# Attention and FFN in one kernel: FFN units as 64-row halves beside the 64-row score matmuls, one run per slot

## Chip, cores and metric

One core of one Trainium2 chip. The metric is the device time of one execution in microseconds (us), median of several runs.

## The reference

```python
scores = q @ k.T / 8 + bias[bucket(|i-j|)]      # B=8, H=8, S=576, D=64
attn   = softmax(scores)
x      = (attn @ v) as [4608, 512]
out    = ((x @ w_a) * (x @ w_b)) @ w_out        # 512 -> 1536 -> 512
```

Scores have a contraction of only 64 (the head size). 576 rows are 4 x 128 and a tail of 64.

## The kernel before

Two heads are one *pair*; the 32 pairs are processed in 32 *slots*. Into each slot are woven *units* of the FFN, each of four full matmuls of 128 rows and 512 columns: unit a (`pa`), unit b (`pb`), and a third of an output tile (`po`).

```python
def qk1(p, t):                      # two heads side by side: rows 0-63 and rows 64-127
    ps = ps_sc.tile([128, 2, 512], FP32, tag="sc")          # 2 buffers, 2 banks each
    for hh in range(2):
        r = slice(64 * hh, 64 * hh + 64)
        nc.tensor.matmul(out=ps[:, hh, :], lhsT=kT_(p, t)[r, :], rhs=qT[r, :, :], start=True, stop=True)

def qk_tail(p):                     # scores of the tails: full 128 rows, the other head padded with zeros
    for t in range(4):
        nc.tensor.matmul(out=ps[:, 0, :]..., lhsT=kT_(p, t), rhs=qTt_(p))            # 128 columns
    nc.tensor.matmul(out=ps[:, 1, :], lhsT=kTt_(p), rhs=qT_(p))                      # 512 columns
    pt = bank(TR if p < R3 else AV)                                                  # small tail scores, 64 columns

# a slot from 12 on ("unit" stands for a share of the slot's nine):
steps = [qk1(s,0)+qk1(s,1), ex(s,0), unit, ex(s,1), av 0-2 of s-1, norm, unit, mul(s,0), unit, mul(s,1),
         av 3-4 of s-1, norm, ..., qk1(s,2)+qk1(s,3), ex(s,2), unit, ex(s,3), unit, mul(s,2), unit, mul(s,3),
         qk_tail(s), ex_tail(s), unit, unit, mul_tail(s), unit]
```

`ex` is the exponential on ScalarE, `mul` the multiplication by the exponentiated bias on VectorE, `av` attention times v, `norm` the reciprocal and the division (`rc`, `XG`) on VectorE. From slot 12 on both av groups and the small tail scores share one bank ("av", one buffer). FFN results take two banks "ffn" and one "tr".

The softmax here doesn't subtract the row's maximum and nothing guards it: scores larger than these inputs give would overflow.

## Time and profile before

| | before |
|---|---|
| median time | 418.04 us (417.79 to 418.82, 4 runs) |
| slot length, slots 12 to 31 | 11.06 us each |
| TensorE busy / ScalarE / VectorE | 98% / 59% / 47% |
| visits to the 64-row form per slot | 2 |

The lines themselves are in the prediction. The view that carries most is the chain of waits: the work that ended last, followed back through what released each piece.

### The profile page before, as it was taken

To read this page: it belongs to the slowest core of one execution; us is meant where nothing else is said; L and a number is where in the kernel's file an instruction comes from. 1 tells how busy PE (TensorE), PEld (TensorE's weight loads), DVE (VectorE), ACT (ScalarE), POOL (GpSimd) and SP (SyncE) were. 2 spreads that over 40 slices of the span, in tenths; PEclk is the share of its full clock that TensorE was granted. 3 is DMA by queue.
4 is the path that set the end of the run, shared out by engine and by line. 5 is a ranking of instruction groups with operands and counts; after the bars stand their busy time and mean duration, and the time that the engine had idled before them with its cause. 6 is when DMAs were issued, how large, how long until landed. Compare 5 with 4: busy or idle time off the path is not lost.

```text
span 415.9 us, 8484 instructions
## 1 busy us (share of the span) xinstructions
PE 406.9 (98%) x3407; PEld 208.1 (50%) x3407; DVE 197.0 (47%) x484; ACT 246.1 (59%) x347; POOL 119.4 (29%) x161
## 2 busy tenths in 40 slices
PE   8799999999999999999999999999999999999996
PEld 3563555555454555554554455555545554444443
DVE  3684666556542555355525563455425540430430
ACT  4887476756656766577666665676567642322321
POOL 9898739903538000920073003000000000000000
PEclk9999999999999999999999999999999999999999
DMA  9999999999939950999099908921120002002004
GB/s 160 190 155 179 159 171 145 183 165 87 140 51 168 176 44 22 155 188 103 16 115 199 124 16 74 177 48 39 41 90 7 11 17 101 2 0 102 2 0 101
DMA packets 164935, 40.75 MB, mean 98 GB/s; under 512 B 155320, under 2 KB 160224, under 8 KB 164896
## 3 DMA queue, kind: packets, MB, share of 16 engines
q0 software_dynamic: 110448, 18.75, 61.9%
q1 hardware_dynamic: 53168, 21.03, 26.8%
q10 hardware_dynamic: 1280, 0.43, 0.5%
q8 instruction: 26, 0.43, 0.4%
q14 instruction: 13, 0.11, 0.1%
HBM read 38.77 MB, written 9.45 MB: 116 GB/s over the span
## 4 chain that ended last, share of the span: by engine, by line
PE 92%; DVE 2%; POOL 2%; DMA 1%; ACT 1%; issue 1%; DVEq 0%; POOLq 0%; ACTq 0%
PE pa L511 23%; PE pb L511 23%; PE po L542 22%; PE av L412 9%; PE qk L342 7%; PE av L403 2%; PE qkt L367 2%; PE qkt L370 2%; DMA W<-bias_tab 1%; DVE XG L449 1%; DVE at L361 1%; PE po L530 1%; PE trx L475 1%; PE qktt L373 0%; PE trq L291 0%
## 5 line engine op out<-in xcount | busy, mean ns | idle before, releaser
L353 ACT ACTIVATE at<-qk 128x1024 bf16<-128x1024 f32 x128 | 125.9, 1023 | 24.4 <-PE qk L342 23.4
L523 DVE TENSOR_TENSOR g<-pb,ha 128x512 bf16<-128x512 f32 x108 | 74.7, 692 | 117.0 <-PE pb L511 102.9
L511 PE MATMUL pa<-xn,wa 128*128 128x512 bf16 x432 | 111.3, 380 | 0.2 <-DVE xn L257 0.2
L511 PE MATMUL pb<-xn,wb 128*128 128x512 bf16 x432 | 111.2, 379 | 0.0
L518 ACT ACTIVATE ha<-pa 128x512 f32<-128x512 f32 x108 | 64.6, 598 | 65.4 <-PE pa L511 64.9
L542 PE MATMUL po<-wo,g 128*128 128x512 bf16 x420 | 98.6, 379 | 0.0
L511 PEld LDWEIGHTS <-wa 128*128 128x128 bf16 x432 | 39.1, 98 | 49.6 <-issue 9.3
L511 PEld LDWEIGHTS <-wb 128*128 128x128 bf16 x432 | 39.2, 98 | 48.1 <-issue 7.6
L361 DVE TENSOR_TENSOR at<-at,W 128x512 bf16<-128x512 bf16 (+1 forms) x128 | 59.1, 484 | 7.7 <-ACT at L353 5.5
L542 PEld LDWEIGHTS <-g 128*128 128x128 bf16 x420 | 37.9, 98 | 46.4 <-issue 7.4
L546 ACT ACTIVATE ob<-po 128x512 f32<-128x512 f32 x35 | 20.9, 597 | 60.7 <-PE po L542 60.7
L123 POOL DMA_DIRECT2D vm<-in_v_dram x32 | 28.2, 924 | 99.4 <-PE av L412 61.2
L412 PE MATMUL av<-vm,at 128*128 128x65 bf16 x992 | 43.5, 193 | 0.0
L412 PEld LDWEIGHTS <-at 128*128 128x128 bf16 x992 | 39.5, 97 | 6.3
L448 DVE RECIPROCAL rc<-av 128x6 f32<-128x6 f32 x64 | 12.0, 188 | 54.9 <-PE av L412 53.1
L403 PE MATMUL av<-vt,att 128*128 128x130 bf16 x156 | 34.7, 222 | 0.0
L381 ACT ACTIVATE att<-qkt 128x1024 bf16<-128x1024 f32 x32 | 32.6, 1020 | 0.0
L449 DVE TENSOR_TENSOR XG<-av,rc 128x384 bf16<-128x384 f32 x64 | 31.4, 491 | 2.4 <-DVE rc L448 0.2
L123 POOL DMA_DIRECT2D qn<-in_q_dram x28 | 24.4, 921 | 24.6 <-PE trq L291 24.6
L123 POOL DMA_DIRECT2D kn<-in_k_dram x28 | 24.5, 913 | 4.9 <-DMA vt<-in_v_dram 2.0
L342 PE MATMUL qk<-QTb,KTb 64*128 64x512 bf16 x160 | 24.2, 381 | 0.0
L403 PEld LDWEIGHTS <-att 128*128 128x128 bf16 x156 | 15.3, 98 | 7.4 <-issue 0.7
(122 smaller groups left out, 243.6 us busy)
## 6 DMA issues: line engine op xcount, KB each, us to landing
out_dram<-ob SPq DMA_DIRECT2D x32, 256.0 KB, 4.1
vm<-in_v_dram POOLq DMA_DIRECT2D x28, 128.0 KB, 5.5
qn<-in_q_dram POOLq DMA_DIRECT2D x24, 128.0 KB, 8.5
kn<-in_k_dram POOLq DMA_DIRECT2D x24, 128.0 KB, 9.3
wa<-in_moe_w_a_dram POOLq DMA_DIRECT2D x3, 512.0 KB, 6.8
wb<-in_moe_w_b_dram POOLq DMA_DIRECT2D x3, 512.0 KB, 9.5
wo<-in_moe_w_out_dram POOLq DMA_DIRECT2D x1, 1536.0 KB, 13.2
W<-bias_tab POOLq DMA_DIRECT2D x4, 192.0 KB, 5.8
```

The lines of the kernel that those rows point to most:

```text
L123: nc.gpsimd.dma_start(out=(vm[b % 2][:, h0:h1, t, 0:Dh] if dst is None else dst[b % 2][:, :].rearrange("p (t h d) -> p t h d", h=H, t=NM)[ ...
L342: nc.tensor.matmul(out=ps[:, hh, :], lhsT=kT_(p, t)[r, :], rhs=qT[r, :, :], start=True, stop=True)
L353: nc.scalar.activation(out=at[:, :, :], in_=ps[:, :, :], func=ACTF.Exp, scale=scale)
L361: nc.vector.tensor_tensor(out=at[:, :, lo:hi], in0=at[:, :, lo:hi], in1=w[:, :, y:(None if z < 0 else z):-1], op=MULT)
L381: nc.scalar.activation(out=at[:, 0:1024].rearrange("p (a x) -> p a x", a=2), in_=ps[:, :, :], func=ACTF.Exp, scale=scale)
L403: nc.tensor.matmul(out=pav[:, slot, :, :], lhsT=x, rhs=vt[b // 2 % 2][:, 4 * i + hp, :, 0:Dh + 1], start=fresh, stop=True, skip_group_chec ...
L412: nc.tensor.matmul(out=pav[:, slot, hh, :], lhsT=x, rhs=vm[i][:, 2 * hp + hh, t, 0:Dh + 1], start=False, stop=True, skip_group_check=True)
L449: nc.vector.tensor_tensor(out=xg[:, j0:j0 + n, :, :], in0=pav[:, 0:n, :, 0:Dh], in1=rc.unsqueeze(3).to_broadcast([128, n, 2, Dh]), op=MULT)
L511: nc.tensor.matmul(out=ff[key][:, :], lhsT=w[df // FW][:, mc, 128 * (df % FW):128 * (df % FW) + 128], rhs=xn_sb[mc][:, xin(c)], start=(i = ...
L518: nc.scalar.activation(out=ha[:, :], in_=ff["pa"][:, :], func=ACTF.Copy)
L523: nc.vector.tensor_tensor(out=g_sb[df][:, :], in0=ff["pb"][:, :], in1=ff["ha"][:, :], op=MULT)
L542: nc.tensor.matmul(out=po[:, :], lhsT=g_sb[df][:, 128 * tt:128 * tt + 128], rhs=wo_sb[:, df, :], start=(df == 0), stop=(df == NDF - 1))
```

## The change

The intent: each change between the full form and the 64-row form of TensorE costs time. If FFN matmuls are themselves cut into 64-row halves, and halves of two different units run side by side, they can stand among the qk pairs without a change of form.

```diff
+    R4 = 14
-    g_sb = [wpool.tile(...) for df in range(NDF)]
+    g_sb = [[wpool.tile(...) for df in range(NDF)] for i in range(2)]     # two sets of activations
     def qk_tail(p):
+        if p >= R4:                        # tails in row halves, no zero half streamed
+            for t in range(NM):
+                for hh in range(2):
+                    nc.tensor.matmul(out=ps[:, hh, 64*t:64*t+64], lhsT=kT_(p, t)[r, :], rhs=qTt_(p)[r, ...])
+            for x in range(2):
+                nc.tensor.matmul(out=ps[:, x, 256:512], lhsT=kTt_(p), rhs=qT_(p)[:, 2*x:2*x+2, :])
...
+    def begin(x, y):                       # unit x rows 0-63 beside unit y rows 64-127
+        for p, q_ in zip(*got):
+            mm(p, lo); mm(q_, hi)
+        nc.vector.tensor_copy(out=hop, in_=got[1][0][0][0:1, 0:1])        # orders the two halves
+    def end(x, y, got):                    # then the other halves
+        for p, q_ in zip(*got):
+            mm(q_, lo, False, True, True); mm(p, hi, False, True, True)
+        u_end(y[0]); u_end(x[0])
+    def run(s, a, b):
+        u, v_ = ((b[0], FF), (a[0], AV)), ((b[1], FF), (a[1], TR))
+        qk1(s, 0); ex(s, 0); got0 = begin(*u)
+        qk1(s, 1); ex(s, 1); got1 = begin(*v_)
+        qk1(s, 2); ex(s, 2); end(*u, got0)
+        qk1(s, 3); ex(s, 3); end(*v_, got1)
...
-    quotas = {4: 12, 5: 7, 6: 6, 7: 4, 8: 4}
+    quotas = {4: 12, 5: 7, 6: 6, 7: 4, 8: 4, 12: 3, 13: 3}               # units of a slot; otherwise 9
+        elif new and s >= R4:
+            c, i = (s - 6) // 4, 3 * ((s - R4) % 4)
+            a, b = [[(kind, c, i + j, 0) for j in range(3)] for kind in "ab"]
+            mine = [u for u in outs if u[1] < c][0:3]                     # empty in slots 16 and 17
+            steps += [run, qk_tail, mine[0:1], ex_tail, mul 0, mine[1:2], mul 1, av 0-2, norm,
+                      a[2:], mul 2, mine[2:], av 3-4, norm, t_x, turns, b[2:], mul 3, mul_tail]
```

(Cuts marked with dots, the last list in short form; there is also one output buffer fewer, three instead of four. `hop` is a copy of one element between the first and the second halves of an accumulation, so that the second come after the first.)

More of the change, by code (lines that the diff above doesn't have):

```diff
@@ L48 @@
     wrk = ctx.enter_context(tc.tile_pool(name="wrk", bufs=2))
-    obp = ctx.enter_context(tc.tile_pool(name="obp", bufs=4))
+    obp = ctx.enter_context(tc.tile_pool(name="obp", bufs=3))
     atp = ctx.enter_context(tc.tile_pool(name="atp", bufs=8))
@@ L115 @@
     xn_sb = [wpool.tile([128, 3 * SM + ST * B], BF16, name=f"xn{mc}") for mc in range(NMC)]
-    g_sb = [wpool.tile([128, DM], BF16, name=f"g{df}") for df in range(NDF)]
+    g_sb = [[wpool.tile([128, DM], BF16, name=f"g{i}_{df}") for df in range(NDF)] for i in range(2)]
     def early(b):
@@ L365, in qk_tail @@
         ps = ps_sc.tile([128, 2, 512], FP32, tag="sc", name=f"qkt{p}")
-        for t in range(NM):
+        if p >= R4:
+            for t in range(NM):
+                for hh in range(2):
+                    r = slice(64 * hh, 64 * hh + 64)
+                    nc.tensor.matmul(out=ps[:, hh, ST * t:ST * t + ST], lhsT=kT_(p, t)[r, :],
+                                     rhs=qTt_(p)[r, ST * hh:ST * hh + ST], start=True, stop=True)
+            for x in range(2):
+                nc.tensor.matmul(out=ps[:, x, 256:512], lhsT=kTt_(p), rhs=qT_(p)[:, 2 * x:2 * x + 2, :],
+                                 start=True, stop=True)
+        for t in range(NM if p < R4 else 0):
             nc.tensor.matmul(
@@ L369, in qk_tail @@
                 lhsT=kT_(p, t), rhs=qTt_(p), start=True, stop=True)
-        nc.tensor.matmul(out=ps[:, 1, :], lhsT=kTt_(p), rhs=qT_(p), start=True, stop=True)
+        if p < R4:
+            nc.tensor.matmul(out=ps[:, 1, :], lhsT=kTt_(p), rhs=qT_(p), start=True, stop=True)
         pt = bank(TR if p < R3 else AV, FP32, f"qktt{p}")
@@ L380, in ex_tail @@
         nc.scalar.activation(out=at[:, 1024:1024 + ST], in_=pt[:, 0:ST], func=ACTF.Exp, scale=scale)
-        nc.scalar.activation(out=at[:, 0:1024].rearrange("p (a x) -> p a x", a=2),
-                             in_=ps[:, :, :], func=ACTF.Exp, scale=scale)
+        if p < R4:
+            nc.scalar.activation(out=at[:, 0:1024].rearrange("p (a x) -> p a x", a=2),
+                                 in_=ps[:, :, :], func=ACTF.Exp, scale=scale)
+        else:
+            nc.scalar.activation(out=at[:, 0:1024].rearrange("p (y a x) -> p a y x", y=2, a=2),
+                                 in_=ps[:, :, :].rearrange("p a (y x) -> p a y x", y=2),
+                                 func=ACTF.Exp, scale=scale)
     def mul_tail(p):
@@ L494 @@
     turn3 = 0
+    here = None
+    hop = const.tile([1, 1], FP32, name="hop")
     def ff_bank(name):
         nonlocal turn3
-        where = FF
-        if ring3:
+        where = here or FF
+        if ring3 and here is None:
             turn3 += 1
@@ L504, with ff_in, mm, a_end @@
     MC = (0, 1, 2, 3)
-    def ff_mm(c, df, w, key, m0, m1):
-        if m0 == 0:
-            ff[key] = ff_bank(f"{key}{c}_{df}")
-        for i in range(m0, m1):
-            mc = MC[i]
-            nc.tensor.matmul(out=ff[key][:, :], lhsT=w[df // FW][:, mc, 128 * (df % FW):128 * (df % FW) + 128],
-                             rhs=xn_sb[mc][:, xin(c)],
-                             start=(i == 0), stop=(i == NMC - 1))
-    def ff_a(c, df, m0=0):
-        ff_mm(c, df, wa_sb, "pa", m0, NMC)
-        ha = wrk.tile([128, 512], FP32, tag="ha", name=f"ha{c}_{df}")
-        nc.scalar.activation(out=ha[:, :], in_=ff["pa"][:, :], func=ACTF.Copy)
-        ff["ha"] = ha
-    def ff_b(c, df, m0=0):
-        ff_mm(c, df, wb_sb, "pb", m0, NMC)
-        nc.vector.tensor_tensor(out=g_sb[df][:, :], in0=ff["pb"][:, :], in1=ff["ha"][:, :], op=MULT)
+    def ff_in(c, df, w, key):
+        if (key, df) not in ff:
+            ff[key, df] = ff_bank(f"{key}{c}_{df}")
+        return [(ff[key, df], w[df // FW][:, mc, 128 * (df % FW):128 * (df % FW) + 128],
+                 xn_sb[mc][:, xin(c)], i == 0, i == NMC - 1) for i, mc in enumerate(MC)]
+    lo, hi = slice(0, 64), slice(64, 128)
+    def mm(x, r=slice(0, 128), start=None, stop=None, go_on=False):
+        o, w, m, first, final = x
+        return nc.tensor.matmul(out=o[:, :], lhsT=w[r, :], rhs=m[r, :],
+                         start=first if start is None else start,
+                                stop=final if stop is None else stop, skip_group_check=go_on)
+    def a_end(c, df):
+        ha = wrk.tile([128, 512], FP32, tag="ha", name=f"ha{c}_{df}")
+        nc.scalar.activation(out=ha[:, :], in_=ff.pop(("pa", df))[:, :], func=ACTF.Copy)
+        ff["ha", df] = ha
+    def b_end(c, df):
+        nc.vector.tensor_tensor(out=g_sb[c % 2][df][:, :], in0=ff.pop(("pb", df))[:, :], in1=ff.pop(("ha", df))[:, :], op=MULT)
     def ff_last(c, tt):
@@ L529, in ff_last @@
             for df in range(NDF):
-                nc.tensor.matmul(out=po[:, cols], lhsT=g_sb[df][:, 128 * tt:128 * tt + 128],
+                nc.tensor.matmul(out=po[:, cols], lhsT=g_sb[c % 2][df][:, 128 * tt:128 * tt + 128],
                                  rhs=wo_sb[:, df, cols], start=(df == 0), stop=(df == NDF - 1))
@@ L535, in ff_last, with ff_out @@
                 eng.dma_start(out=out[r0:r0 + ST, cols], in_=ob[64 * hh:64 * hh + 64, cols])
-    def ff_o(c, tt, part):
+    def ff_out(c, tt, part):
         if part == 0:
-            ff["po"] = ff_bank(f"po{c}_{tt}")
-        po = ff["po"]
-        for df in range(4 * part, 4 * part + 4):
-            nc.tensor.matmul(out=po[:, :], lhsT=g_sb[df][:, 128 * tt:128 * tt + 128],
-                             rhs=wo_sb[:, df, :], start=(df == 0), stop=(df == NDF - 1))
-        if part == 2:
-            ob = obp.tile([128, DM], FP32, tag="ob", name=f"ob{c}_{tt}")
-            nc.scalar.activation(out=ob[:, :], in_=po[:, :], func=ACTF.Copy)
-            if c < B:
-                r0 = S * c + 128 * tt
-                nc.sync.dma_start(out=out[r0:r0 + 128, :], in_=ob[:, :])
-            else:
-                for hh in range(2):
-                    r0 = S * (2 * tt + hh) + SM
-                    nc.sync.dma_start(out=out[r0:r0 + ST, :], in_=ob[64 * hh:64 * hh + 64, :])
+            ff["po", tt] = ff_bank(f"po{c}_{tt}")
+        return [(ff["po", tt], g_sb[c % 2][df][:, 128 * tt:128 * tt + 128], wo_sb[:, df, :], df == 0, df == NDF - 1)
+                for df in range(4 * part, 4 * part + 4)]
@@ new lines, in o_end @@
+    def o_end(c, tt, part):
+        if part < 2:
+            return
+        po = ff.pop(("po", tt))
+        ob = obp.tile([128, DM], FP32, tag="ob", name=f"ob{c}_{tt}")
+        nc.scalar.activation(out=ob[:, :], in_=po[:, :], func=ACTF.Copy)
+        if c < B:
+            r0 = S * c + 128 * tt
+            nc.sync.dma_start(out=out[r0:r0 + 128, :], in_=ob[:, :])
+        else:
+            for hh in range(2):
+                r0 = S * (2 * tt + hh) + SM
+                nc.sync.dma_start(out=out[r0:r0 + ST, :], in_=ob[64 * hh:64 * hh + 64, :])
@@ L555 @@
     units = []
-    def last(part):
-        if part == 0:
-            ff_last(NCH - 1, 3)
     for c in range(NCH):
         for df in range(NDF):
-            m0 = 3 if c == 0 and df == 0 else 0
-            units.append(lambda c=c, df=df, m0=m0: ff_a(c, df, m0))
-            units.append(lambda c=c, df=df, m0=m0: ff_b(c, df, m0))
+            units.append(("a", c, df, 0))
+            units.append(("b", c, df, 0))
         for tt in range(4):
             for part in range(3):
-                if c == NCH - 1 and tt == 3:
-                    units.append(lambda part=part: last(part))
-                else:
-                    units.append(lambda c=c, tt=tt, part=part: ff_o(c, tt, part))
+                units.append(("o", c, tt, part))
@@ L571, with u_mms, u_end @@
     nxt = 0
+    def u_mms(u):
+        kind, c, i, part = u
+        if kind == "o":
+            return ff_out(c, i, part)
+        mms = ff_in(c, i, wa_sb if kind == "a" else wb_sb, "pa" if kind == "a" else "pb")
+        return mms[3:] if c == 0 and i == 0 else mms
+    def u_end(u):
+        kind, c, i, part = u
+        if kind == "a":
+            a_end(c, i)
+        elif kind == "b":
+            b_end(c, i)
+        else:
+            o_end(c, i, part)
     def put_units(n):
@@ L575, in put_units, with put_in @@
         for _ in range(n):
-            units[nxt]()
+            u = units[nxt]
             nxt += 1
+            if u[0] == "o" and u[1] == NCH - 1 and u[2] == 3:
+                if u[3] == 0:
+                    ff_last(NCH - 1, 3)
+                continue
+            for x in u_mms(u):
+                mm(x)
+            u_end(u)
+    def put_in(us, where):
+        nonlocal here
+        for u in us:
+            here = where
+            for x in u_mms(u):
+                mm(x)
+            here = None
+            u_end(u)
+    def begin(x, y):
+        nonlocal here
+        got = []
+        for u, where in (x, y):
+            here = where
+            got.append(u_mms(u))
+        here = None
+        for p, q_ in zip(*got):
+            mm(p, lo)
+            mm(q_, hi)
+        nc.vector.tensor_copy(out=hop[:, :], in_=got[1][0][0][0:1, 0:1])
+        return got
+    def end(x, y, got):
+        for p, q_ in zip(*got):
+            mm(q_, lo, False, True, True)
+            mm(p, hi, False, True, True)
+        u_end(y[0])
+        u_end(x[0])
+    def run(s, a, b):
+        u, v_ = ((b[0], FF), (a[0], AV)), ((b[1], FF), (a[1], TR))
+        qk1(s, 0)
+        ex(s, 0)
+        got0 = begin(*u)
+        qk1(s, 1)
+        ex(s, 1)
+        got1 = begin(*v_)
+        qk1(s, 2)
+        ex(s, 2)
+        end(*u, got0)
+        qk1(s, 3)
+        ex(s, 3)
+        end(*v_, got1)
     ACT = nc.scalar
@@ L714 @@
     norm(3, 3)
-    ff_mm(0, 0, wa_sb, "pa", 0, 3)
+    for x in ff_in(0, 0, wa_sb, "pa")[0:3]:
+        mm(x)
     t_x(3, AV, range(3))
     t_x(3, AV, range(3, 5))
-    ff_mm(0, 0, wb_sb, "pb", 0, 3)
+    for x in ff_in(0, 0, wb_sb, "pb")[0:3]:
+        mm(x)
     copy(ACT, xn_sb[3][:, 0:384], st[3]["x"][:, 0:384])
@@ L737, in turns @@
             turn(b, "qkt"[s % 4])
-    quotas = {4: 12, 5: 7, 6: 6, 7: 4, 8: 4}
+    quotas = {4: 12, 5: 7, 6: 6, 7: 4, 8: 4, 12: 3, 13: 3}
+    outs = None
+    every = list(units)
     for s in range(4, NP + 1):
@@ L745 @@
         steps = []
+        if s == R4:
+            outs = [("o", c, tt, part) for c in range(1, NCH) for tt in range(4) for part in range(3)]
+            outs = outs[3 * (R4 - R3):]
         if s == R3:
@@ L754 @@
                       lambda: t_k(5, AV), lambda: c_k(5), U, U]
+        elif new and s >= R4:
+            c, i = (s - 6) // 4, 3 * ((s - R4) % 4)
+            a, b = [[(kind, c, i + j, 0) for j in range(3)] for kind in "ab"]
+            mine = [u for u in outs if u[1] < c][0:3]
+            outs = outs[len(mine):]
+            steps += [lambda: run(s, a, b), lambda: qk_tail(s), lambda: put_in(mine[0:1], FF), lambda: ex_tail(s),
+                      lambda: mul(s, 0), lambda: put_in(mine[1:2], FF), lambda: mul(s, 1), A(0, 1, 2), N(0),
+                      lambda: put_in(a[2:], TR), lambda: mul(s, 2), lambda: put_in(mine[2:], FF), A(3, 4), N(3),
+                      lambda: t_x(s - 1), lambda: turns(s), lambda: put_in(b[2:], FF),
+                      lambda: mul(s, 3), lambda: mul_tail(s)]
         elif new:
@@ L780 @@
         quota = quotas.get(s, 9)
+        if s == NP:
+            c, i = (s - 6) // 4, 3 * ((s - R4) % 4)
+            units = [u for u in outs if u[1] < c] + [u for u in units if u[1] == c and u[0] < "o" and u[2] >= i]
+            units += [u for u in outs if u[1] == c]
+            for d in range(c + 1, NCH):
+                units += [u for u in every if u[1] == d]
+            nxt = 0
         seen, put = 0, 0
```

## The prediction

> **What bounds the kernel now.** I read the page first (busy shares, slices, chain), then the chain of waits between two head-pair slots, then the timelines of the four engines there.
>
> ```profile
> PE 406.9 (98%) x3407; PEld 208.1 (50%) x3407; DVE 197.0 (47%) x484; ACT 246.1 (59%) x347; POOL 119.4 (29%) x161
> ...
> PE   8799999999999999999999999999999999999996
> ...
> PE 92%; DVE 2%; POOL 2%; DMA 1%; ACT 1%; issue 1%; DVEq 0%; POOLq 0%; ACTq 0%
> ```
>
> TensorE is busy 98% of the span, from the third slice to the last but one, and 92% of the chain that ended last is TensorE. The busy share alone proves little, because the recorded matmuls overlap (a 512-column matmul is recorded as 379 ns, but the next starts 216 ns later). So I turn to the chain, whose pieces are start-to-start times. This is one slot (one pair of heads plus nine FFN units), slot 14:
>
> ```profile
> 138.47 0.54 PE qk L342 x4
> 139.01 0.97 PE pa L511 x4
> ...
> 140.03 0.24 PE av L412 x8
> ...
> 143.20 0.54 PE qk L342 x4
> 143.74 0.97 PE pb L511 x4
> 144.71 0.86 PE pa L511 x4
> ...
> 146.44 0.22 PE qkt L367 x4
> 146.66 0.22 PE qkt L370
> 146.88 0.06 PE qktt L373 x2
> ...
> 149.53 0.54 PE qk L342 x4
> ```
>
> Columns: start, length, what. Every piece is PE, with nothing of another engine between: in this stretch TensorE waits for nobody. A slot lasts 149.53 - 138.47 = 11.06 us, and the other slots up to 31 begin at the same 11.06 us step. A unit of four full matmuls costs 0.86 (4 x 0.216), but 0.97 when it follows qk: 0.11 is lost. The four qk matmuls run as two concurrent 64-row pairs, which should cost 2 x 0.216 = 0.43, and cost 0.54: again 0.11. So each visit to the 64-row form costs 0.21-0.22 us, and a slot has two of them.
>
> The other engines in the same slot (timelines: start, length, engine, line, what; in brackets the idle time before):
>
> ```profile
> 142.64 0.60 ACT L518 ACTIVATE ha<-pa 128x512 f32<-128x512 f32 x1 [1.12 <-PE pa L511]
> 143.57 1.94 ACT L353 ACTIVATE at<-qk 128x1024 bf16<-128x1024 f32 x2 [0.33 <-PE qk L342]
> ...
> 146.97 0.22 ACT L380 ACTIVATE att<-qktt 128x64 bf16<-128x64 f32 x1 [0.76 <-PE qktt L373]
> 147.09 1.02 ACT L381 ACTIVATE att<-qkt 128x1024 bf16<-128x1024 f32 x1
> ```
> ```profile
> 140.91 0.20 DVE L448 RECIPROCAL rc<-av 128x6 f32<-128x6 f32 x1 [1.64 <-PE av L412]
> 141.14 0.56 DVE L449 TENSOR_TENSOR XG<-av,rc 128x384 bf16<-128x384 f32 x1
> 141.85 0.69 DVE L523 TENSOR_TENSOR g<-pb,ha 128x512 bf16<-128x512 f32 x1
> 142.46 0.88 DVE L361 TENSOR_TENSOR at<-at,W 128x512 bf16<-128x512 bf16 x2
> ```
>
> Both have gaps, so neither bounds. What I take from them: exps of 1.02 us follow each other at 0.92 (1.94 for two), so an instruction overlaps the next by about 0.1; the av bank is free about 1.1 us after the last av matmul (av 0-2 streams until 140.87 on the chain's clock, the last matmul starting near 140.68; reciprocal at 140.91, XG to 141.70); an exp starts 0.43 us after its qk pair (records: qk at 143.14, exp at 143.57).
>
> **What the Trainium skill says.** "TensorEngine Tiling (Array Packing)", Key Properties: changing the tiling mode, not just the tile, drains the engine. The trace agrees: 0.11 us on each side. "TensorE: Matmul & The Clock Gate", Part 3: matmuls in different row groups run concurrently, their starts some 4 ns apart. The trace agrees: qk x4 of 512 columns takes 0.54, not 0.86. "Perfetto Trace Analysis", Identifying the Most-Contended Engine, says that matmul busy time is a poor measure because matmuls are pipelined; this trace shows it (379 ns recorded, 216 from start to start). "TensorEngine Tiling (Array Packing)", Gotcha 1, says that different row tiles cannot access the same PSUM bank at once; the change gives each half of a pair its own bank, as qk already does, and no run here shows the other case.
>
> **The change, part by part** (18 slots, 14 to 31).
>
> 1. One visit to the 64-row form per slot instead of two. The run is qk, four unit pairs, qk, four, qk, four, qk, four, and the tail's 64-row part follows directly; then comes full form until the next run. Units in halves: 16 full matmuls become 32 halves = 16 concurrent pairs at 0.216, the same array time (that a pair keeps 0.216 in a run of 20 is taken from runs of two; nothing in this trace is longer). Saved: 18 x 0.21 = 3.8 us.
>
> 2. Tail scores: four full matmuls with zero-padded heads (0.22) become four concurrent pairs of 64 columns. Matmuls of 64-65 columns start 0.03 apart (av x8 in 0.24, qktt x2 in 0.06), so four pairs take 0.13 if pairs overlap, 0.24 if the weight loads do not. The 512-column one becomes two of 256: the same. Saved: up to 18 x 0.09 = 1.7 us; I take 1.6.
>
> So TensorE's own work would give 418.2 - 5.4 = 412.8, with steady slots of 11.06 - 0.30 = 10.76.
>
> 3. What comes back as waits. The units are redistributed: slots 12 and 13 get three instead of nine, slots 16 and 17 have six (no output unit is allowed while the previous chunk is used up), the rest go to the end, which is TensorE alone at the same 0.86 a unit. Moving work costs nothing, but the thin slots lose their filler.
>
> Slots 12 and 13, from the order of the changed program: av 0-2 is followed at once by av 3-4 in the same single av bank. Before, two units (1.73 us) stood between. Now TensorE waits for reciprocal and XG: about 1.05. Further, the second qk of slot 13 needs the buffer of slot 12's tail exp: qk at 0, unit 0.54, av 1.4, wait to 3.35, av 3-4, qk at 4.05, exp 2 at 4.5, exp 3 at 5.4, tail exps 6.3 to 7.4; slot 13 starts at about 7.0 and its second qk waits 0.2. Another 0.1 for the tail's own buffer. Sum: 2 x 1.15 + 0.2 = 2.5 us. (Slots of about 7.0 to 7.2 instead of 5.9.)
>
> Slots 16 and 17, from the run's start at 0: qk at 0, 1.09, 2.17, 3.25, run's end 4.33, tail to 4.83. Exps start 0.43, 1.52, 2.60; copy of a at 3.50; exp 3 at 3.98; second copy 4.88; the small tail exp 5.36 to 5.58, since it is queued behind them. It holds the av bank, and with no output unit between, av 0-2 stands at 4.83 and waits to 5.63: 0.8. Then VectorE (g at 5.5, two multiplies, reciprocal at 6.9, XG to 7.7) frees the bank at 7.75 for av 3-4, which is there at 7.4: 0.35. Sum: 2 x 1.15 = 2.3 us.
>
> Normal slots: the first output unit takes the bank of the first b, free when g of it is done: copy 3.50 to 4.10, g 4.13 to 4.82, seen at 4.87; TensorE is there at 4.83 to 4.93. 0 to 0.05 a slot, 0.3 us in all. The hop (a one-element copy that orders the two halves of an accumulation): VectorE has g, multiply and two tail multiplies of the slot before until about 1.7, so the hop is done near 1.9; the second halves begin at 2.39. Hidden. The av bank for a of the run: XG of av 3-4 ends about when the run begins, 0.25 before its use. Hidden, barely.
>
> Start of slot 32: av follows the last unit of slot 31 directly and needs the last multiply behind g: about 0.7.
>
> Sum: 418.2 - 5.4 + 2.5 + 2.3 + 0.3 + 0.7 = 418.6. I round towards the side of the intent, since waits that I placed at their worst may partly overlap with slack I do not see: 418.0.
>
> **The rivals.**
> - No waits of weight: the thin slots run dense, all 5.4 us arrive: 412.8. For it: the kernel before has no wait in 18 slots, its author places banks with care. Against it: the order in the changed program puts av 3-4 right behind av 0-2 with one bank, and the chain from av through XG is 1.1 us in this profile.
> - A new wait in every slot (hop late, b's bank late, av bank late): 0.2 to 0.5 a slot, 3.6 to 9 us on top: 422 to 427. For it: two of the margins above are under 0.3 us, and every slot repeats them. Against it: both are positive by my working, and VectorE and ScalarE are busy only about 60% of a slot.
> - Halves do not overlap fully in a long run (weights not loaded in time, or two banks accumulating at once): each pair that lost 0.05 would cost 20 x 0.05 x 18 = 18 us; fully serial, 18 x 16 x 0.216 = 62 us. For it: qk pairs only ever write, and only two pairs stand in a row. Against it: the second pair's weights are loaded while the first streams (0.22 from pair to pair).
>
> **Range and chances.** The saving is firm to about 0.6, the waits of the thin slots to about 2, the per-slot margins may go wrong by 0.1 to 0.2 x 18 = 2 to 3.5, upwards more than downwards. So 418.0, with 414.5 to 421.5 for 8 in 10. Faster by over 2% means under 409.8, below what TensorE's work allows: 0.02. Slower by over 2% means above 426.6, which needs the second or third rival in full: 0.05. Within 2%: 0.93.
>
> **What would show it.** In the changed profile: qk tiles of a slot 1.08 apart in one run; a lost 0.11 only before the first and after the tail; slots of 10.76 (18 to 30), about 9.3 (16, 17) and 7.0 to 7.2 (12, 13); in the chain of waits, DVE (XG) and ACT (the small tail exp) in those four slots alone. Slots of 10.76 but 12, 13, 16 and 17 without waits would mean the first rival; slots over 10.9, the second; pairs over 0.22 apart, the third. I am wrong outright if the time leaves 414.5 to 421.5.

## The result, and the profile after

The changed kernel takes 418.75 us (median of 418.50, 418.58, 418.92, 420.04) against 418.04: ratio 1.002, 95% interval 0.9995 to 1.0045. A second comparison (run after_again, on chip 8) gave 418.54 against 418.15, ratio 1.0015, interval 0.9996 to 1.0035. Within 2%, and not told apart from no change at all.

The 420.04 us are the profiled run. It lost its time at the start, where both kernels do the same work: slot 12 begins at 117.62 us, against 116.28 before. Most of it, 0.93, was lost in slot 7, where TensorE waits for a load of k; the second profile of the same kernel (run after_again) has no such wait and begins slot 12 at 116.10. The list of waits of TensorE:

```profile
PE av L419 <- DVE XG L465: 2.1, 4, 0.9
PE av L419 <- ACT att L391: 1.4, 2, 0.7
...
PE trk L312 <- DMA kn<-in_k_dram: 0.7, 2, 0.4
```

(Columns: who waited for whom, us in total, times, longest.) From slot 12 to the end it takes 300.51 us, against 299.66 before: that is the comparison to explain, +0.85. (The second profile of the changed kernel has 300.54.) The two upper lines are new: av waits for XG four times (slots 12, 13, 16, 17) and for the small tail exp twice (slots 16, 17). Neither line stands in the list of before.

The page of the changed kernel, engines and chain:

```profile
PE 399.6 (96%) x3724; PEld 211.0 (50%) x3785; DVE 200.7 (48%) x520; ACT 244.5 (58%) x347; POOL 119.4 (29%) x161
...
PE 87%; DVE 4%; DMA 3%; POOL 2%; ACT 2%; issue 2%; DVEq 0%; POOLq 0%; ACTq 0%
```

TensorE's part of the chain fell from 92 to 87%; VectorE's rose from 2 to 4 and ScalarE's from 1 to 2. (DMA's 3% goes with the late start of this run: the second profile has PE 89%, DVE 4%, ACT 2%, DMA 1%.) And 3724 matmuls stand against 3785 weight loads: 61 records are missing, two in each ordinary slot and one in every 10.8 us of the plain FFN stretch at the end, so that "x3" appears in the chain where four ran. Such a hole makes one step of 0.43 out of two of 0.216 and stands in the chain as a piece of "issue", mostly 0.05; a wait it is not.

An ordinary slot, slot 22, in the chain of waits (start, length, what):

```profile
215.58 0.32 PE qk L343 x2
215.91 0.21 PE pb L534
216.12 0.00 PE pa L534
...
216.77 0.22 PE qk L343 x2
...
218.93 0.22 PE qk L343 x2
...
220.01 0.12 PE qkt L371 x8
220.12 0.33 PE qkt L374 x2
220.45 0.06 PE qktt L384 x2
220.51 0.27 PE po L534
220.77 0.05 issue
220.83 1.46 PE po L534 x6
```

Halves of pb and pa start together (0.21 and 0.00), the qk tiles stand 1.08 apart, and the form changes once: 0.32 instead of 0.22 at the first qk, 0.33 instead of 0.22 after the tail. The tail's eight halves take 0.12, where four padded matmuls took 0.22. The next slot begins at 226.38: 10.80 us, where it was 11.06. A part of the saving, 0.05, is waited away in front of the first matmul of po, for the bank that g of the first b still reads: in the timelines this g ends at 220.34, and po starts at 220.40, 0.08 after the last qktt matmul where 0.03 is usual. (The 0.05 of "issue" behind it is a missing record.)

And the places where the time went. Slot 12, between the two av groups:

```profile
119.85 0.26 PE av L428 x8
120.11 0.02 issue
120.13 0.21 DVE rc L464
120.34 0.02 issue
120.36 0.57 DVE XG L465
120.93 0.05 issue
120.98 0.23 PE av L419
```

The chain leaves TensorE for VectorE and comes back. In the timeline the next av group starts 1.08 us after the last matmul of the group before, where 0.03 is usual: 1.05 us lost, because both groups need the one av bank. Slot 16, from the end of the run on:

```profile
158.10 0.04 PE pb L534
158.14 0.49 ACT at L354
158.63 0.50 ACT ha L540
...
159.16 0.69 DVE g L544
159.85 0.58 DVE at L362 x2
...
160.57 0.20 DVE rc L464
...
160.79 0.57 DVE XG L465
161.35 0.05 issue
161.40 0.23 PE av L419
```

For 3.3 us TensorE is not on the chain at all. It has work in this time, but the end is set by the exp, the copy of a, g, two multiplies and the normalisation in a row. In the timeline av 0-2 waits 0.85 us (for the small tail exp) and av 3-4 waits 0.35 (for XG). The start of slot 32:

```profile
323.69 0.69 DVE g L544
324.38 0.34 DVE at L362
324.73 0.05 issue
324.77 0.33 PE av L428 x5
```

Here av waits for the last multiply, which stands behind g on VectorE; two shorter waits (0.12 before, 0.18 after) stand beside it.

The account from slot 12 on, all from slot starts in the two traces:

| slots | before | after | without waits | effect |
|---|---|---|---|---|
| 14, 15, 18 to 31 (nine units) | 11.06 | 10.80 (slot 14: 10.87) | | 16 x -0.26, + 0.07: -4.1 |
| 12, 13 (three units) | 11.06 with nine | 7.03, 7.31 | 11.06 - 6 x 0.864 = 5.88 | +2.6 |
| 16, 17 (six units) | 11.06 with nine | 9.35, 9.36 | 11.06 - 3 x 0.864 = 8.47 in the old form | +1.8 |
| start of 32 | waits of 0.18 | 0.12 + 0.48 + 0.18 | | +0.6 |

Sum +0.9, measured +0.85.

### The profile page after: what moved, and what is told of

The parts are those of the page before. It is cut to its first block, busy times and chain, and to the rows that moved or that the text cites. A ratio compares the mean times of both kernels' runs of the same rounds, so it can differ in the third digit from the quotient of the medians.

```text
span 418.1 us, 9240 instructions
## 1 busy us (share of the span) xinstructions
PE 399.6 (96%) x3724; PEld 211.0 (50%) x3785; DVE 200.7 (48%) x520; ACT 244.5 (58%) x347; POOL 119.4 (29%) x161
## 4 chain that ended last, share of the span: by engine, by line
PE 87%; DVE 4%; DMA 3%; POOL 2%; ACT 2%; issue 2%; DVEq 0%; POOLq 0%; ACTq 0%
PE pa L534 22%; PE pb L534 22%; PE po L534 21%; PE av L428 8%; PE qk L343 7%; PE av L419 2%; DMA kn<-in_k_dram 1%; DMA W<-bias_tab 1%; DVE XG L465 1%; PE qkt L374 1%; DVE at L362 1%; ACT at L354 1%; PE po L551 1%; PE trx L491 1%; PE qkt L377 1%
## 5 line engine op out<-in xcount | busy, mean ns | idle before, releaser
L354 ACT ACTIVATE at<-qk 128x1024 bf16<-128x1024 f32 x128 | 128.4, 1028 | 35.2 <-PE qk L343 32.4
L534 PE MATMUL pa<-xn,wa 128*128 128x512 bf16 (+1 forms) x568 | 147.0, 378 | 0.6 <-DVE xn L258 0.2
L534 PE MATMUL pb<-xn,wb 128*128 128x512 bf16 (+1 forms) x551 | 143.4, 377 | 1.3
L534 PE MATMUL po<-wo,g 128*128 128x512 bf16 x396 | 97.5, 379 | 1.5 <-issue 0.3
L534 PEld LDWEIGHTS <-wa 64*128 64x128 bf16 (+1 forms) x576 | 52.8, 96 | 45.0 <-issue 2.9
L534 PEld LDWEIGHTS <-wb 64*128 64x128 bf16 (+1 forms) x576 | 52.8, 96 | 43.5 <-issue 3.4
L534 PEld LDWEIGHTS <-g 128*128 128x128 bf16 x420 | 39.3, 98 | 43.5 <-issue 2.5
L343 PE MATMUL qk<-QTb,KTb 64*128 64x512 bf16 x160 | 30.1, 379 | 0.1
L396 ACT ACTIVATE att<-qkt 128x1024 bf16<-128x1024 f32 x18 | 19.3, 1071 | 0.0
```

What stands on the lines that cost most here:

```text
L354: nc.scalar.activation(out=at[:, :, :], in_=ps[:, :, :], func=ACTF.Exp, scale=scale)
L396: nc.scalar.activation(out=at[:, 0:1024].rearrange("p (y a x) -> p a y x", y=2, a=2), in_=ps[:, :, :].rearrange("p a (y x) -> p a y x", y= ...
L534: return nc.tensor.matmul(out=o[:, :], lhsT=w[r, :], rhs=m[r, :], start=first if start is None else start, stop=final if stop is None else ...
```

## The experiments

The theory (T): the form saves about 0.26 us in each ordinary slot, and the schedule that it needs gives it back in slots 12, 13, 16, 17 and at the start of 32. Rivals: the long run and the hop cost what the changes of form saved (R1); or the waits of the thin slots only use up slack, and removing them moves them (R2). Every kernel gave the right result. Times are medians of the fast runs. "T" or "R1" after a result says which of them it bears out.

All kernels do the same work up to slot 12, so the traces can be compared from there to the end, free of the spread of the first part (us):

| run | slot 12 to the end | against before | against the changed kernel |
|---|---|---|---|
| before | 299.66 | | |
| changed kernel, two profiles | 300.51, 300.54 | +0.85 | |
| old form | 304.79 | +5.13 | +4.28 |
| thin slots in before | 302.52 | +2.86 | |
| four visits more | 313.94 | | +13.43 |
| tail in full form | 301.27 | | +0.76 |
| row-halved tail in before | 301.62 | +1.96 | |
| fill 12, 13 | 299.08 | | -1.43 |
| free 16, 17 | 298.95 | | -1.56 |
| first in 32 | 299.70 | | -0.81 |
| all repairs | 295.72 | -3.94 | -4.79 |

### The old form in the new schedule

```diff
-        qk1(s, 0) .. begin(*u) .. qk1(s, 1) .. begin(*v_) .. qk1(s, 2) .. end .. qk1(s, 3) .. end
+        qk1(s, 0); ex(s, 0); qk1(s, 1); ex(s, 1); both(*u)      # full matmuls, then the two ends
+        qk1(s, 2); ex(s, 2); qk1(s, 3); ex(s, 3); both(*v_)
     # and qk_tail, ex_tail in the form of before for all slots
```

> The changed kernel's order of units and slots, but with qk in two groups of two pairs, full 128-row units and the full tail: the form of before in the schedule of after. Theory T (the form saves about 0.26 us in each of slots 14 to 31, the schedule gives it back in slots 12, 13, 16, 17 and at the start of 32): 18 x 0.26 to 0.30 slower than the changed kernel, 423.2 to 424.2 us, slots of about 11.06. Rival R1 (long 64-row runs and the hop cost what the mode changes saved, so the form is worth nothing): within 1 us of the changed kernel, 418 to 419.7.

Measured: 422.80 us, ratio to before 1.0107 (1.008 to 1.0135); the changed kernel had 1.002 and 1.0015. So the form is worth about 0.9% or 4 us, and the schedule alone costs about 1.1%: T, not R1. It came out 0.4 us under the range that I had given, since in slots 16 and 17 the form saves nothing: they last 9.29 in the old form and 9.35 in the new. There the chain over ScalarE and VectorE sets the length, whatever TensorE saves. Ordinary slots have 11.06 again, so the output buffer that was given up costs nothing there:

```profile
204.56 0.54 PE qk L344 x4
205.10 0.97 PE pb L535 x4
...
206.93 0.54 PE qk L344 x4
```

### The thin slots alone, in the kernel before

```diff
-    quotas = {4: 12, 5: 7, 6: 6, 7: 4, 8: 4}
+    quotas = {4: 12, 5: 7, 6: 6, 7: 4, 8: 4, 12: 3, 13: 3}
```

> The kernel before with one edit: slots 12 and 13 put three units instead of nine, the rest moves to the end. T: TensorE waits about 1.05 us for XG in each of the two slots and some 0.4 more at tail buffers, so 2.3 to 2.7 us slower than before, 420.4 to 420.8; slots 12 and 13 of 7.0 to 7.3. R2 (the waits of the thin slots only use up slack, work done later fills it): within 0.7 us of before.

Measured: 420.68 us against 417.69 (ratio 1.0056, 1.0031 to 1.0081). Slots 12 and 13 last 7.03 and 7.31, to 0.01 us as in the changed kernel, and slot 14 11.34: another 0.28 is waited for the tail's buffer, which the run of the changed kernel covers. T. Units moved to the end do not give the time back. The loss, 3.0 us by the medians and 2.86 in the traces, is a little over the 2.3 to 2.7 expected: the waits at the tails' buffers came to about 0.75, not 0.4.

### Four visits more

```diff
-        begin / end in halves between the qk pairs
+        for i, (x, y) in enumerate((u, v_)):
+            qk1(s, 2*i);     ex(s, 2*i);     put_mm(*x)      # full matmuls
+            qk1(s, 2*i + 1); ex(s, 2*i + 1); put_mm(*y)
+            u_end(y[0]); u_end(x[0])
```

> The changed kernel with full 128-row units between the four qk pairs, so that a slot visits the 64-row form five times (four qk, tail) instead of once; no hop. T: each visit costs 0.21 us, so a slot is 4 x 0.21 - 0.05 = 0.79 longer, about 11.6, and the whole 12.5 to 14 us slower than the changed kernel, 431 to 433. R1 (it is the halves and the hop that cost, not the visits): under 3 us slower, or faster.

Measured: 431.74 us, ratio 1.0326 (1.0309 to 1.0343). Slots of 11.60, that is +0.80 for four visits, and the wait of 0.05 gone: 0.21 per visit. The chain shows the two sides of each:

```profile
207.74 0.32 PE qk L343 x2
208.06 0.97 PE pb L534 x4
209.03 0.32 PE qk L343 x2
209.35 0.97 PE pa L534 x4
```

0.32 for 0.22 going in and 0.97 for 0.86 coming out. T; the halves and the hop are not what costs.

### The tail in full form

```diff
+    RT = NP                               # in qk_tail and ex_tail, in place of R4
-        if p >= R4:
+        if p >= RT:
```

> The changed kernel with the tail scores in full 128-row form again, the run in halves kept. T: TensorE's tail grows by 0.10 us a slot (0.22 for 0.12), of which 0.05 was waited away at the first output unit anyway, and slots 16 and 17 wait for ScalarE: slots of 10.85 instead of 10.80, 0.7 to 1.0 us slower than the changed kernel in all. R1 (the tail's row halves save nothing): the same time, slots of 10.80.

Measured: 419.24 us, ratio 1.003 (1.0015 to 1.0045), slots of 10.85. So the tail's row halves save 0.10 on TensorE, of which 0.05 arrives; 0.05 goes into the wait for the bank of po. The difference of the medians (0.5 to 0.7 us against the two measurements of the changed kernel) has the size of the noise and lies at or under the range expected; the slots and the traces (0.76) are the evidence.

### The tail's row halves alone, in the kernel before

```diff
# kernel before; qk_tail and ex_tail of the changed kernel for p >= 14, nothing else
```

> The kernel before with the tail scores alone in row halves (slots 14 to 31). T: 0.10 saved and one more visit at 0.21, so 0.11 a slot, slots of 11.17, 1.7 to 2.2 us slower than before, 419.8. R1 (the mode change is not what costs): 1.8 us faster.

Measured: 419.75 us, ratio 1.0042 (1.0024 to 1.006), slots of 11.17 instead of 11.06. The same edit that saves inside the run costs 0.11 outside it: it saves 0.10 and pays for one more visit, 0.21. T.

### Slots 12 and 13: more work between the two av groups

```diff
-            if s >= R3:
-                steps += av34
             steps += [lambda: qk(s, 2), lambda: ex(s, 2), U]
+            if s >= R3:
+                steps += av34
```

> The changed kernel with av 3-4 of slots 12 and 13 moved behind the second qk group and a unit. T: the wait of 1.05 for XG goes in both slots, 1.8 to 2.1 us faster than the changed kernel, about 416.7; slots 12 and 13 of about 6.0 to 6.3. R2 (the wait only moves to the next buffer, ScalarE being nearly full in these slots): under 0.8 us faster.

Measured: 416.95 us, ratio to before 0.9971 (0.9946 to 0.9997). The slots last 6.36 and 6.57, not 6.0 to 6.3: 1.4 us gained, not 1.8 to 2.1. My number was off, and the chain says where:

```profile
120.43 0.19 DVE rc L464
120.63 0.02 issue
120.65 0.43 DVE XG L465
121.08 0.05 issue
121.13 0.23 PE qktt L384 x2
```

The small tail scores also want the av bank, and av 3-4 now stands right before them: a new wait of 0.47 and 0.46. In this piece R2 was right: a part of the wait moved to the next user of the same bank. ScalarE was not nearly full, as the expectation has it for R2: in the changed kernel it is busy 4.46 of 7.02 us in slot 12 and 5.30 of 7.31 in slot 13.

### Slots 16 and 17: another bank for the small tail scores

```diff
-        pt = bank(TR if p < R3 else AV, FP32, ...)
+        pt = bank(TR if p < R3 else FF if p in (16, 17) else AV, FP32, ...)
+            if not mine:      # norm of av 0-2 ahead of mul 0 and mul 1
+                steps += [run, qk_tail, ex_tail, av 0-2, norm, mul 0, mul 1, a[2:], mul 2, av 3-4, ...]
```

> The changed kernel with the small tail scores of slots 16 and 17 in an FFN bank instead of the av bank, and the normalisation ahead of two multiplies. T: of 1.15 us of waits in each slot about 0.35 stays, 1.4 to 1.7 us faster than the changed kernel, about 417.1; slots 16 and 17 of about 8.55. R2 (the wait moves to the FFN bank or to the next slot's run): under 0.6 us faster.

Measured: 417.23 us, ratio 0.9973 (0.9948 to 0.9997); slots 16 and 17 last 8.55 and 8.58 instead of 9.35 and 9.36. T, to 0.03 us a slot. The edit changes two things, the bank and the place of the normalisation; no run separates them.

### Slot 32: units first

```diff
-            steps += [av 0-2, norm, U, av 3-4, norm, U, t_x, c_x, U, U, U, U, U, U, U]
+            steps += [U, av 0-2, norm, U, U, av 3-4, norm, U, t_x, c_x, U, U, U, U, U]
```

> The changed kernel with two more FFN units ahead of av in slot 32 (taken from the end of the same slot). T: the waits of 0.12, 0.48 and 0.18 us at that place go, 0.6 to 0.8 us faster than the changed kernel, 417.9. R2 (the wait reappears at the next buffer): no change.

Measured: 417.70 us, ratio 0.9992 (0.9979 to 1.0006). In the trace the three waits are gone. By the medians it is 0.8 to 1.05 us faster than the changed kernel, by the traces 0.81 (0.6 to 0.8 expected): T.

### All repairs together

The three edits above, and the small tail scores of slots 12 and 13 in an FFN bank too:

```diff
+        pt = bank(TR if p < R3 else FF if p in (12, 13, 16, 17) else AV, FP32, ...)
```

> The changed kernel with the three repairs together (av 3-4 of slots 12 and 13 later, small tail scores of slots 12, 13, 16 and 17 in an FFN bank, units first in slot 32). T: 1.4 + 0.9 (the bank wait of 0.46 that the first repair ran into, twice) + 1.6 + 0.8 = 4.7 us faster than the changed kernel, about 414.0, 0.9 to 1.1% faster than before; slots 12 and 13 of 5.9 and 6.15, 16 and 17 of 8.55, others 10.80. R2 (repairs overlap, or waits reappear): 415.5 or more.

> The changed kernel as it is, on the same chip as the repaired one: 418.3 to 419.0, 0.1 to 0.3% slower than before in both theories. It gives the repaired kernel its comparison within one chip.

Measured on one chip: 413.72 us (413.42 to 414.56) with the repairs, 418.54 without, 418.15 before. The ratio to before is 0.9897 (0.988 to 0.9914): 1.0% faster than before, while the changed kernel has 1.0015. Slots 12 and 13 last 5.88 and 6.10, slots 16 and 17 8.55 and 8.58, the others 10.80. The chain through slot 12 is TensorE alone again; the only gap in these lines, 0.05 of issue before "x2", is a missing record:

```profile
118.78 0.54 PE qk L343 x4
119.31 0.32 PE po L534
119.64 0.05 issue
119.69 0.59 PE po L534 x2
120.28 0.06 PE av L419
...
120.88 0.22 PE qkt L377 x4
```

The gain of 4.8 us over the changed kernel is what the waits add up to, less what stays: about 0.35 in each of slots 16 and 17 and 0.22 in slot 13, where the second qk still waits. This is the best kernel.

## Why the prediction was right, point by point

- **Bound and cost of a visit.** Right. 0.21 per visit was read from pieces of 0.54 and 0.97; the kernel with five visits per slot measured it again, at 0.21.
- **Units in halves cost the same array time.** Right. qk tiles 1.08 apart are one qk pair and four unit pairs at 0.216. The prediction had called this an assumption, having seen runs of two pairs only; it holds in runs of 20 that accumulate.
- **Tail.** Right: 0.12 measured for 0.13 worked out.
- **Saving per slot.** 0.30 worked out for TensorE, 0.26 arrived. The rest, 0.04 to 0.05, is the wait for the first output unit's bank, which the prediction had at 0 to 0.05, so 16 slots x 0.05 = 0.8 us where it booked 0.3. The kernel with the full tail shows that wait taking up half of what the tail saves.
- **Slots 12 and 13.** 2.5 us of waits predicted, 2.6 measured: 1.05 for XG was 1.05, and the 0.2 for the second qk of slot 13 was 0.27.
- **Slots 16 and 17.** Waits of 0.8 and 0.35 predicted, 0.85 and 0.35 in the trace (9.35 us per slot where 9.3 was predicted).
- **Slot 32.** About 0.7 predicted, 0.6 measured.
- **Hop and av bank in the run.** Predicted hidden; the list of waits of TensorE has neither.
- **The last step failed in direction.** The sum was 418.6. I took 0.6 off, "since waits that I placed at their worst may partly overlap with slack I do not see". There was no such slack: every wait came in full. So a gain of 0.2 was forecast (418.0 from 418.2), and the kernel lost 0.4 to 0.7 by the medians, 0.85 in the traces. That the measured 418.54 and 418.75 sit on the sum is partly luck: the sum had a loss of 0.4, the traces have 0.85, nearly all of the difference being the wait of 0.05 in ordinary slots; and it started from 418.2, a little above the later medians of before (418.04, 418.15).
- **Two slips in the working, without effect.** 18 x 0.09 is 1.6, not 1.7 (1.6 was booked). By its own readings (140.68 and 141.70) the av bank is free 1.02 us after the start of the last av matmul, not 1.1 (1.05 was booked).
- **The rivals.** A run without waits (412.8) needed the bank chains not to bind, and they bind; with them repaired the kernel comes to 413.7. A new wait in every slot came, but of 0.05. Halves that do not overlap did not come.

What stays open: whether the waits that are left in the best kernel (about 0.35 us in each of slots 16 and 17, 0.22 in slot 13, 0.05 in ordinary slots) can be removed too. No run tried it.

## What to carry to other kernels

When an engine is the bound and runs without a gap, a saving on it arrives only where its filler work stays in place. Write down, for each slot that the new schedule makes thinner, which single buffer its next instruction needs and how long the chain that frees it is (here 1.05 us through reciprocal and division), and place at least that much work in between. A trick such as the row-halved tail is worth what it saves less the change of form around it: the same edit gave 0.10 inside a run and cost 0.11 alone. And when a sum of read durations gives a number, do not shade it towards the intent of the change.

## What the Trainium skill lacked or had wrong

- "TensorEngine Tiling (Array Packing)", Key Properties: it says that a change of tiling mode drains the engine, with no figure. Here 0.10 to 0.11 us going in and 0.11 coming out, 0.21 per visit in runs with one, two, three and five visits per slot.
- "TensorE: Matmul & The Clock Gate", Part 3, measures packing with four row tiles of 32 (3.07 times). No measured figure stands there for two row groups of 64: here two 512-column halves take 0.216 us from pair to pair, the same as one full matmul of 128 rows, so the whole factor of two, in runs of 20 pairs, also where the two accumulate into different banks.
- The same page, Back-to-back issue gap, gives about 131 ns per matmul of 512 columns and 81 ns at 128 columns as a sustained rate in real kernels. Here 216 ns (four in 0.86 us) and 56 ns (four in 0.22 us): its formula for the isolated gap, N/2.4 + 2.5 ns, is the one that fits.
- No page says that matmul records can be missing at regular distances in a trace (61 of 3785 here, each making one step of 0.43 us out of two of 0.216); the count of weight loads beside that of matmuls shows it.
